# Gated long convolution and token MLP: the second forward transform stage in 64x32 tiles, the first in row pairs, and one shuffle per row pair

## The chip, the cores and the metric

The kernel runs on one core of one Trainium2 chip. The metric is the device time of one execution in microseconds; lower is better. Of several runs the median is given. The profile is of one further execution, and its span (first to last instruction on the core) is a little shorter than its device time.

## The reference, cut to what matters

S = 2048 positions, D = 448 channels, F = 1792, one batch, bf16 inputs.

```python
def A(q, k, v, shift_k, ssm_k, ssm_D):
    k_pad = pad(k, 3 rows in front)
    k_shift = sum(k_pad[:, t:t + S, :] * shift_k[:, 3 - t] for t in range(4))
    kv = k_shift * v
    kv_f = rfft(pad(kv, to 2 * S), along S)
    kf_f = rfft(pad(ssm_k, to 2 * S), along S)
    y = irfft(kv_f * kf_f)[:S].astype(bf16)
    return q * (y + kv * ssm_D)

def B(x, w1, b1, w2, b2):
    h = layernorm(x)                               # over D
    u = gelu(einsum("bsd,sf->bdf", h, w1) + b1)    # mixes positions
    return transpose(einsum("bdf,fs->bds", u, w2) + b2)

h = x + A(layernorm(x), k, v, shift_k, ssm_k, ssm_D)     # x is A_q
out = h + B(layernorm(h), w1, b1, w2, b2)
```

## The kernel before

The sequence is laid out as 128 partitions by R = 16 rows: position 16 q + r sits in partition q, row r. The long convolution is done as a transform of length 4096 in two forward stages, a product, and two inverse stages, all as matmuls with tables of sines (`E`, `FW`, `MA`, `MB`, `MN`, `ET`). DB is the 896 bytes of one row of 448 bf16 channels.

In order of the data: `emit_kT` transposes the filter `ssm_k` into `KT`; `emit_kv` does the short convolution (transposes L947, matmuls L973, and a multiply by v on DVE, L988) and leaves kv in `V`. `emit_stage1` (L1030) runs once for the filter (tag k, from KT) and once for kv (tag u, from V). For each group i of four rows it makes four frequency quarters `jh`. For one quarter eight matmuls (L1040) of 128x32 weights go to the four column tiles of the array, one row per tile, the two parts x (real and imaginary) to two PSUM banks; a bank pair of 128x896 is then copied to SBUF by ACT or DVE (L1050; L1048 for the first group of k, where `DR` adds the coefficient ssm_D to the filter's transform). After every second quarter three DMAs (L1056) move the result from partitions that stand for (row, frequency) to the layout of stage 2: partitions 0 to 31 and 96 to 127 by POOL, 32 to 95 by SP. They write half of the columns of 32 partitions of `TK` or `TU`.

`emit_stage2` (L1067) takes two frequency columns j at a time. For each part h it has four matmuls of 128x64 weights (L1075), two column tiles, and the bank pair goes back into T in place (`evac`, L719 on ACT and L722 on DVE without a scale, L720 and L723 with the scale of the k path). `emit_products_i1` multiplies the two transforms on DVE (L1108, 128x1792) and does the first inverse stage (L1120) with two row tiles; its result is evacuated to TU, and DMAs (L1144, and L1133 for the last pair) shuffle it back to `TZ`. `emit_i2` (L1240 and the normalisation after it) and `emit_mlp` (L1365, L1375, L1387) follow. `emit_warm` and `dummy` (L1154, L1006) are matmuls whose result is not used. BN statistics of q (L1180, L1182) are computed on DVE in between, and small steps of the normalisation on POOL (L1185, L1188, L1197).

The order of work is set by a planner in the kernel (`_Sched`). Every step of a stage has a rank, written out by hand in `WHEN`; an engine takes, of the operations that are ready in the planner's own clock, the one with the lowest rank. `WHERE` names for each evacuation that may run on either engine whether it is ACT, DVE, or left to the planner. The resulting order is then fixed in the program of each engine, and semaphores hold each instruction until its operands are there. PSUM's eight banks are handed out in pairs; the results of stage 1 go through a ring of buffers (`gring`) in the regions of `MR` and `X`, and the load of q into X waits for the last shuffle of u.

The lines of before that the change touches most:

```python
for i in range(R // 4):                       # stage 1, L1032
    for jh in range(4):
        c0 = 64 * (jh & 1) + 32 * (jh >> 1)
        for x in range(2):
            for q, r in enumerate((4 * i, 4 * i + 2, 4 * i + 1, 4 * i + 3)):
                ...
for h in range(2):                            # stage 2, L1070
    for c in range(2):
        for par in range(2):
            j = 2 * jj + par
            ... FW[:, 64 * c:64 * c + 64], T[:, j, h, :] -> PS[64 * par:64 * par + 64, b.slots[c]]
```

Of the kernel before, what the change touches and what calls it, by code (L numbers as in the profile page):

```python
# [12 lines left out]
    "dummy": (283,),  # L13
    "tables": (138, 234, 288, 20, 81, 325, 139, 217,),
    "loads": (91, 107, 134, 143, 231, 216, 80, 297, 0, 238, 183, 285, 228, 299, 145,),
    "kv": (290, 148, 151, 174, 63, 282, 100, 192, 205, 47, 18, 112, 141, 45, 207, 160, 233,),
    "kT": (201, 13, 14, 175, 200, 130, 54, 53,),
    "k1": (132, 135, 152, 226, 122, 144, 165, 213, 68, 51, 154, 167, 89, 168, 262, 336,),
    "k2": (23, 150, 83, 97, 224, 227, 140, 153, 258, 248, 180, 195, 169, 219, 338, 235,),
    "u1": (71, 86, 116, 123, 46, 82, 176, 221, 117, 215, 261, 316, 173, 184, 277, 278,),  # L20
    "xload": (156, 298, 314, 302,),
    "bias": (75, 171,),
    "q": (271, 208, 318, 93, 268, 185, 279, 280, 264,),
    "u2": (133, 142, 220, 210, 241, 249, 64, 114, 159, 196, 137, 189, 1, 115, 252, 251,),
    "i1": (179, 121, 99, 3, 190, 96, 186, 149, 188, 240, 203, 202, 128, 92, 212, 95,),
    "ct": (36, 187, 87, 300,),
    "xn": (257, 17, 6, 222, 161, 317,),
    "w1a": (329, 239, 230, 55,),
    "w1b": (306,),
    "warm": (291, 307, 265, 27, 292, 147, 330, 320, 5, 304, 270, 38, 19, 315, 284, 62, 333, 327, 105, 118, 191, 295,  # L30
        324, 259, 56, 8, 332, 113, 236, 273, 206, 198, 182, 274,),
    "i2": (260, 69, 103, 39, 15, 31, 293, 28, 108, 242, 90, 84, 88, 331, 22, 197, 204, 33, 110, 237, 164, 323, 256,
        310, 73, 214, 223, 170, 44, 79, 157, 177, 16, 211, 328, 281, 131, 250, 4, 247, 158, 294, 109, 40, 29, 104,
        34, 243, 267, 129, 98, 287, 70, 178, 67, 162, 246, 120, 155, 2, 125, 11, 229, 42, 253, 272, 59, 124, 119,
        266, 12, 78, 194, 276, 127, 41, 313, 10, 102, 61, 255, 21, 37, 66, 24, 232, 199, 321, 312, 76, 308, 296, 52,
        111, 303, 163, 319, 58, 65, 339, 209, 26, 326, 337, 289, 85,),
    "w2": (146,),
    "mlp": (218, 57, 136, 126, 77, 30, 25, 48, 60, 9, 305, 72, 166, 245, 301, 172, 50, 181, 418, 419, 420, 421, 422,
        423, 424, 425, 426, 427, 428, 429, 430, 431, 432, 433, 434, 435, 436, 437, 438, 439,),
}  # L40
WHERE = {
    "kv": "ddaffffa",
    "kT": "fadfdddd",
    "k1": "fafaafaffaff",
    "k2": "dfdffadaafdafada",
    "u1": "fffaafadaaddafaa",
    "bias": "a",
    "u2": "fdaafafaaaaadafa",
    "i1": "affadfaaffdaffaf",
    "ct": "ffda",  # L50
    "xn": "aaff",
    "i2": "aaffaadafddf",
# [518 lines left out]
def _build(nc, A_q, A_k, A_v, A_shift_k, A_ssm_k, A_ssm_D, B_w1, B_b1, B_w2, B_b2, out):  # L571
# [5 lines left out]
    Bsz, S, D = A_q.shape  # L577
    F = B_w1.shape[1]
    assert Bsz == 1 and S == 2048 and D == 448 and F == 1792 and A_shift_k.shape[-1] == 4
    R = 16  # L580
    NFC = F // 128
    EPS = 1e-5
    DB = 2 * D
# [42 lines left out]
    with ctx:  # L626
# [47 lines left out]
        o_GR = (o_WR, o_WR + 8 * DB, o_X, o_X + 8 * DB)  # L674

        def GR_(s):
            return view(o_GR[s], [R // 4, 2, D])
# [13 lines left out]
        gring = _Pool(4)  # L691
# [36 lines left out]
        def emit_tables():  # L728
# [47 lines left out]
            op("pool", lambda e, W: e.iota(chi, [[0, 2], [1, 4], [0, 16]], base=0, channel_multiplier=0),  # L776
               w=[(o_gc + 512, 512)], n=128, est=190.0)
            for a, b_, c_ in ((0, 112, 14), (112, 128, 2)):
                op("pool", lambda e, W, a=a, b_=b_, c_=c_: e.iota(gcm[:, a:b_], [[0, 8], [512, c_]], base=512 * 14 * (a > 0),
                                                                 channel_multiplier=0),  # L780
                   w=[(o_gc + 1536 + 4 * NB, 512, "gm")], n=128, est=190.0)
                op("pool", lambda e, W, a=a, b_=b_, c_=c_: e.iota(chm[:, a:b_], [[0, 2], [1, 4], [0, c_]], base=0,
                                                                 channel_multiplier=0),
                   w=[(o_gc + 2048 + 4 * NB, 512, "cm")], n=128, est=190.0)
            for k, (b0, st_) in enumerate(((2048, -2048), (2048, 2048), (0, 2048))):
                for a, b_ in (((0, 128),) if k == 0 else ((0, 112), (112, 128))):
                    op("pool", lambda e, W, k=k, b0=b0, st_=st_, a=a, b_=b_: e.iota(
                        cph[:, 128 * k + a:128 * k + b_], [[st_, 2], [0, (b_ - a) // 2]], base=b0, channel_multiplier=0),
# [8 lines left out]
            fields = ((5, 12), (0, 2048), (9, 3), (7, 15), (7, 15), (11, 3), (13, 1), (11, 2))  # L797
# [66 lines left out]
        def emit_loads():  # L864
# [11 lines left out]
            for i, (src, c) in enumerate((("k", 3), ("k", 0), ("v", 0), ("k", 1), ("v", 1), ("k", 2), ("v", 2), ("v", 3))):  # L876
# [9 lines left out]
            op(Dq, lambda e, W: e.dma_start(DR[0:16, :], A_ssm_D.rearrange("(a d) -> a d", a=1).broadcast_to([16, D])),  # L886
               w=[(o_DR, DB)], dmab=16 * DB)
# [142 lines left out]
        def emit_stage1(src, o_src, T, o_T, tag):  # L1030
            shuf[tag] = []
            for i in range(R // 4):  # L1032
                g = _Buf(gring)
                for jh in range(4):
                    sch.t0 = T_K1 + T_DK1 * (4 * i + jh) if tag == "k" else T_U1 + T_DU1 * (4 * i + jh)
                    b = _Buf(psum, 2)
                    c0 = 64 * (jh & 1) + 32 * (jh >> 1)
                    for x in range(2):
                        for q, r in enumerate((4 * i, 4 * i + 2, 4 * i + 1, 4 * i + 3)):
# [13 lines left out]
                    if jh % 2 == 0:  # L1053
                        continue
                    for q_, a, nu in (("pool", 0, 8), ("pool", 96, 8), ("sp", 32, 16)):
                        shuf[tag].append(op(q_, lambda e, W, g=g, i=i, a=a, nu=nu, jh=jh: e.dma_start(  # L1056
                            T[a + i:a + i + 4 * nu - 3:4].rearrange("p (j k) c d -> p j k c d", k=4)[:, :, jh - 1:jh + 1]
                            .rearrange("p j k c d -> p j (k c d)"),
                            GR_(g.slots[0])[a:a + 4 * nu, jh - 1:jh + 1].rearrange("p k c d -> p (k c d)")),
                           br=[g], w=[(o_T + (4 * j + jh - 1) * 2 * DB, 4 * DB, tag) for j in range(4)],  # L1060
                           dmab=4 * nu * 4 * DB, keng=nu, rate=350.0))
# [5 lines left out]
        def emit_stage2(T, o_T, scale):  # L1067
            for jj in range(R // 2):
                bs = [_Buf(psum, 2) for _ in range(2)]
                for h in range(2):  # L1070
                    sch.t0 = (T_K2 if scale else T_U2) + T_D2 * (2 * jj + h)
                    for c in range(2):
                        for par in range(2):
                            j = 2 * jj + par
                            op("pe", lambda e, W, b=bs[h], h=h, j=j, c=c, par=par: e.matmul(  # L1075
                                PS[64 * par:64 * par + 64, b.slots[c], 0:D], FW[:, 64 * c:64 * c + 64], T[:, j, h, :],
                                start=True, stop=True),
                               r=r_fw + [(o_T + (2 * j + h) * DB, DB)], bw=[bs[h]], n=D, est=94.5, mode=2)
                for h in range(2):
                    i = 2 * jj + h  # L1080
# [17 lines left out]
        def emit_products_i1():  # L1098
            for jj in range(R // 2):
                ms = []  # L1100
                for h in range(2):
                    i = 2 * jj + h
                    sch.t0 = T_I1 + T_DI1 * i
# [12 lines left out]
                for h in range(2):  # L1116
# [7 lines left out]
                    evac(lambda jj=jj, h=h: TU[:, 2 * jj:2 * jj + 2, h, :], lambda b=bs[h]: Ppair(b),  # L1124
# [325 lines left out]
```

## Time and profile before

| | |
|---|---|
| device time, median of 3 runs | 179.49 us (178.26, 179.49, 179.64) |
| device time of the profiled execution | 178.13 us |
| span of the profiled execution | 175.9 us |
| granted TensorE clock | 1.000 throughout |
| busy: PE, DVE, ACT, POOL | 166.1, 102.0, 92.2, 63.3 us |
| stage 1 evacuations on ACT, L1050 | 24, 919 ns each |
| products, L1108 | 16, 1080 ns each |
| POOL issues of stage-1 shuffles, L1056 | 32, 553 ns each |
| stage 1 matmuls, L1040 | 256, from 13.7 to 43.2 us |
| stage 2 matmuls, L1075 | 128, from 36.0 to 66.8 us |
| inverse stage 1 matmuls, L1120 | 128, from 53.6 to 73.0 us |

The busy time of PE is taken from matmuls that overlap and whose ends are modelled, so 94% of the span is not the peak of the array; the time from one matmul's start to the next tells more. An evacuation is one ACT or DVE instruction that reads two PSUM banks; successive ones overlap a little, so the distance between their starts is somewhat less than the mean duration. A DMA issue counts as busy on POOL, and for SP it stands in the queue's own record (SPq).

### The profile page before, as it was taken

How to read it: one execution, taken by the hardware profiler on the slowest of the kernel's cores; microseconds unless marked ns; L12 is line 12 of the kernel's file. 1: busy time of each engine (PE TensorE's matmuls, PEld its weight loads, DVE VectorE, ACT ScalarE, POOL GpSimd, SP SyncE). 2: the span in 40 equal slices, each digit the busy share in tenths (PEclk: the TensorE clock that was granted, in tenths of full speed). 3: DMA queues.
4: the chain of work that ended last, by engine and by line, in shares of the span. 5: the costliest groups of instructions: out<-in, count | busy, mean ns of one | idle time of the engine just before them, and what ended most of it. 6: DMA issues, size and time to landing. Idle time of an engine off the chain costs nothing.

```text
span 175.9 us, 3619 instructions
## 1 busy us (share of the span) xinstructions
PE 166.1 (94%) x1445; PEld 95.6 (54%) x1445; DVE 102.0 (58%) x189; ACT 92.2 (52%) x131; POOL 63.3 (36%) x157
## 2 busy tenths in 40 slices
PE   6999999879979999998999999999999999999994
PEld 2786745342323333644544455555557777777784
DVE  6995696848999999998998860000001231331331
ACT  3799958888979999966982656412120000000000
POOL 8576628670600643894888760000000000000000
PEclk9999999999999999999999999999999999999999
DMA  5999855992849386569999999910000111011111
GB/s 174 416 334 332 268 165 201 325 352 71 250 98 383 110 214 198 167 179 390 383 396 405 421 419 417 419 77 0 0 4 0 52 52 52 16 40 52 52 52 52
DMA packets 15444, 35.13 MB, mean 200 GB/s; under 512 B 3820, under 2 KB 9484, under 8 KB 15428
## 3 DMA queue, kind: packets, MB, share of 16 engines
q1 hardware_dynamic: 12164, 28.00, 43.4%
q0 software_dynamic: 3072, 6.80, 12.6%
q8 instruction: 11, 0.18, 0.4%
q10 hardware_dynamic: 192, 0.11, 0.2%
q14 instruction: 5, 0.04, 0.1%
HBM read 22.05 MB, written 1.84 MB: 136 GB/s over the span
## 4 chain that ended last, share of the span: by engine, by line
PE 68%; ACT 10%; POOL 7%; DMA 7%; DVE 4%; issue 2%; DVEq 0%; POOLq 0%
PE ps L1387 24%; PE ps L1375 12%; PE ps L1365 9%; ACT arena L719 8%; DMA arena<-arena 7%; PE ps L1040 4%; PE ps L1006 3%; POOL arena L1056 3%; PE ps L947 3%; PE ps L1240 3%; PE ps L1075 2%; PE ps L1019 2%; PE ps L973 2%; PE ps L1120 2%; DVE arena L1259 1%
## 5 line engine op out<-in xcount | busy, mean ns | idle before, releaser
L1390 DVE SCALAR_TENSOR_TENSOR arena<-ps,arena 128x448 bf16<-128x448 f32 (+2 forms) x17 | 11.1, 656 | 57.4 <-PE ps L1387 57.4
L1387 PE MATMUL ps<-arena 128*128 128x448 bf16 (+2 forms) x238 | 42.7, 342 | 0.0
L1387 PEld LDWEIGHTS ps<-arena 128*128 128x128 bf16 x238 | 33.3, 145 | 9.5
L719 ACT CAST arena<-ps 128x896 bf16<-128x896 f32 (+1 forms) x29 | 23.4, 948 | 1.2 <-PE ps L1075 1.1
L1365 PE MATMUL ps<-arena 128*128 128x448 bf16 x112 | 22.9, 353 | 0.4 <-DVE arena L1318 0.4
L1056 POOL DMA_DIRECT2D arena<-arena x32 | 17.5, 553 | 14.1 <-ACT arena L1050 12.9
L1050 ACT CAST arena<-ps 128x896 bf16<-128x896 f32 x24 | 20.3, 919 | 3.8 <-PE ps L1040 3.5
L1375 PE MATMUL ps<-arena 128*128 128x448 bf16 x112 | 21.8, 353 | 0.0
L1075 PE MATMUL ps<-arena 128*64 128x448 bf16 x128 | 15.8, 360 | 3.4 <-DMA arena<-arena 1.8
L1355 ACT ACTIVATE arena<-ps,arena 128x448 bf16<-128x448 f32 x14 | 8.6, 633 | 19.4 <-PE ps L1375 17.7
L1108 DVE TENSOR_TENSOR arena<-arena 128x1792 bf16<-128x1792 bf16 x16 | 16.7, 1080 | 0.2
L1365 PEld LDWEIGHTS ps<-arena 128*128 128x128 bf16 x112 | 10.6, 98 | 11.5 <-DVE arena L1318 2.5
L1375 PEld LDWEIGHTS ps<-arena 128*128 128x128 bf16 x112 | 10.9, 98 | 10.2
L1040 PE MATMUL ps<-arena 128*32 128x448 bf16 x256 | 15.3, 356 | 0.4 <-DVE arena L988 0.3
L1120 PE MATMUL ps<-arena 64*128 64x448 bf16 x128 | 14.0, 352 | 1.0 <-ACT arena L719 0.9
L1144 POOL DMA_DIRECT2D arena<-arena x14 | 8.2, 588 | 17.4 <-ACT arena L719 16.6
L1075 PEld LDWEIGHTS ps<-arena 128*64 128x64 f16 x128 | 5.7, 108 | 12.8 <-ACT arena L719 3.6
L1287 ACT ACTIVATE arena<-arena 128x448 bf16<-128x448 f32 x14 | 8.0, 575 | 5.9 <-DVE arena L1259 5.7
L988 DVE TENSOR_TENSOR arena<-ps,arena 128x512 bf16<-128x512 f32 (+1 forms) x16 | 9.0, 617 | 2.7 <-PE ps L973 2.7
L1120 PEld LDWEIGHTS ps<-arena 64*128 64x128 f16 x128 | 5.1, 94 | 9.5 <-ACT arena L719 5.0
L719 ACT COPY arena<-ps 128x1024 bf16<-128x1024 bf16 (+1 forms) x9 | 8.9, 1019 | 0.9 <-PE ps L1154 0.6
L1040 PEld LDWEIGHTS ps<-arena 128*32 128x32 f16 x256 | 5.1, 95 | 7.8 <-DVE arena L988 1.9
(94 smaller groups left out, 207.0 us busy)
## 6 DMA issues: line engine op xcount, KB each, us to landing
arena<-in_B_w_dram SPq DMA_DIRECT2D x8, 896.0 KB, 12.0
arena<-in_B_w_dram SPq DMA_DIRECT2D x2, 2048.0 KB, 17.1
arena<-arena SPq DMA_DIRECT2D x16, 224.0 KB, 3.7
arena<-arena POOLq DMA_DIRECT2D x32, 112.0 KB, 3.8
arena<-in_B_w_dram SPq DMA_DIRECT2D x2, 1536.0 KB, 18.7
arena<-arena POOLq DMA_DIRECT2D x14, 196.0 KB, 4.6
arena<-in_A_k_dram SPq DMA_DIRECT2D x4, 448.0 KB, 5.7
arena<-in_A_v_dram SPq DMA_DIRECT2D x4, 448.0 KB, 9.0
```

The costliest lines, as they stand in the source:

```text
L719: return e.copy(out=dst(), in_=src())
L988: return e.tensor_tensor(out=v, in0=u.rearrange("p t (r d) -> p t r d", d=64), in1=v, op=ALU.mult)
L1040: op("pe", lambda e, W, b=b, r=r, q=q, x=x, c0=c0: e.matmul(PS[32 * q:32 * q + 32, b.slots[x], 0:D], E[:, 2 * r + x, c0:c0 + 32], src[:, r ...
L1050: return e.copy(out=dst, in_=Ppair(b)) if W == "act" else e.tensor_copy(out=dst, in_=Ppair(b))
L1056: shuf[tag].append(op(q_, lambda e, W, g=g, i=i, a=a, nu=nu, jh=jh: e.dma_start(T[a + i:a + i + 4 * nu - 3:4].rearrange("p (j k) c d -> p ...
L1075: op("pe", lambda e, W, b=bs[h], h=h, j=j, c=c, par=par: e.matmul(PS[64 * par:64 * par + 64, b.slots[c], 0:D], FW[:, 64 * c:64 * c + 64], ...
L1108: op("dve", lambda e, W, m=m, i=i: e.tensor_tensor(out=MR(m.slots[0]).rearrange("p (x y) d -> p x y d", x=2), in0=TU[:, i].unsqueeze(2).br ...
L1120: k = op("pe", lambda e, W, b=bs[h], m=ms[h], par=par, t=t, tab=tab, xy=xy, P=P: e.matmul(Pb(b, par), tab[P, :], MR(m.slots[0])[P, xy, :], ...
L1365: op("pe", lambda e, W, r=r, fc=fc, b=bs[fc]: e.matmul(Pb(b), W1A[:, r, 128 * fc:128 * fc + 128], Q[:, r, :], start=(r == 0), stop=(r == R ...
L1375: op("pe", lambda e, W, r=r, fc=fc, b=b: e.matmul(Pb(b), W1B[:, r, 128 * (fc - n0):128 * (fc - n0) + 128], Q[:, r, :], start=(r == 0), sto ...
L1387: op("pe", lambda e, W, r=r, fc=fc, b=b, d0=d0, d1=d1: e.matmul(Pb(b)[:, d0:d1], W2[fc // 7][:, fc % 7, r:S:R], G[:, fc, d0:d1], start=(fc ...
L1390: op("dve", lambda e, W, r=r, b=b, A=A, d0=d0, d1=d1: e.scalar_tensor_tensor(out=X[:, r, d0:d1], in0=Pb(b)[:, d0:d1], scalar=bm[:, r:r + 1 ...
```

## The change

Stage 1 takes rows in pairs (i of eight). The four column tiles now hold two rows in two frequency halves, and two quarters `jh` finish a pair. One DMA per row pair moves all 128 partitions at once to sixteen partitions of T, at steps of eight, over all columns; even pairs go by SP, odd ones by POOL. The ring has eight buffers of half the size. Stage 2 pairs column jj with jj + 8. Each matmul takes 64 partitions and 32 weight columns, so that eight tiles (two row tiles, four column tiles) hold the two columns, the two parts h and the two halves t. The products and the inverse stage follow the new numbering, the tables get their constants for it, `DR` is filled in two places (one more DMA), and `WHEN` and `WHERE` are new lists.

```diff
 WHEN = {
...
-    "k1": (132, 135, 152, 226, 122, 144, 165, 213, 68, 51, 154, 167, 89, 168, 262, 336,),
-    "k2": (23, 150, 83, 97, 224, 227, 140, 153, 258, 248, 180, 195, 169, 219, 338, 235,),
-    "u1": (71, 86, 116, 123, 46, 82, 176, 221, 117, 215, 261, 316, 173, 184, 277, 278,),
+    "k1": (105, 154, 129, 182, 62, 181, 50, 124, 223, 242, 99, 102, 188, 200, 127, 227,),
+    "k2": (90, 337, 244, 245, 296, 297, 247, 264, 47, 5, 79, 72, 211, 246, 204, 89,),
+    "u1": (210, 259, 217, 243, 27, 91, 73, 132, 100, 183, 117, 164, 144, 163, 190, 209,),
...
-        o_GR = (o_WR, o_WR + 8 * DB, o_X, o_X + 8 * DB)
+        o_GR = tuple(o + 4 * DB * s for o in (o_WR, o_X) for s in range(4))
...
-        gring = _Pool(4)
+        gring = _Pool(8)
...
-            op(Dq, lambda e, W: e.dma_start(DR[0:16, :], A_ssm_D.rearrange("(a d) -> a d", a=1).broadcast_to([16, D])),
-               w=[(o_DR, DB)], dmab=16 * DB)
+            for h in range(2):
+                op(Dq, lambda e, W, h=h: e.dma_start(DR[64 * h:64 * h + 16, :],
+                                                     A_ssm_D.rearrange("(a d) -> a d", a=1).broadcast_to([16, D])),
+                   w=[(o_DR, DB, "dr")], dmab=16 * DB)
...
-            for i in range(R // 4):
+            for i in range(R // 2):
                 g = _Buf(gring)
-                for jh in range(4):
+                pi = 4 * (i & 1) + (i >> 1)
+                for jh in range(2):
...
                     b = _Buf(psum, 2)
-                    c0 = 64 * (jh & 1) + 32 * (jh >> 1)
                     for x in range(2):
-                        for q, r in enumerate((4 * i, 4 * i + 2, 4 * i + 1, 4 * i + 3)):
+                        for q in range(4):
+                            r = 2 * i + (q & 1)
+                            c0 = 64 * ((q >> 1) ^ x) + 32 * jh
...
-                    if jh % 2 == 0:
-                        continue
-                    for q_, a, nu in (("pool", 0, 8), ("pool", 96, 8), ("sp", 32, 16)):
-                        shuf[tag].append(op(q_, lambda e, W, g=g, i=i, a=a, nu=nu, jh=jh: e.dma_start(
-                            T[a + i:a + i + 4 * nu - 3:4].rearrange("p (j k) c d -> p j k c d", k=4)[:, :, jh - 1:jh + 1]
-                            .rearrange("p j k c d -> p j (k c d)"),
-                            GR_(g.slots[0])[a:a + 4 * nu, jh - 1:jh + 1].rearrange("p k c d -> p (k c d)")),
-                           br=[g], w=[(o_T + (4 * j + jh - 1) * 2 * DB, 4 * DB, tag) for j in range(4)],
-                           dmab=4 * nu * 4 * DB, keng=nu, rate=350.0))
+                q_ = ("sp", "pool")[i & 1]
+                shuf[tag].append(op(q_, lambda e, W, g=g, pi=pi: e.dma_start(
+                    T[pi:pi + 121:8].rearrange("p (j k) c d -> p j (k c d)", k=2),
+                    GR_(g.slots[0]).rearrange("p k c d -> p (k c d)")),
+                   br=[g], w=[(o_T, 32 * DB, tag)], dmab=128 * 4 * DB, rate=350.0))
...
                 bs = [_Buf(psum, 2) for _ in range(2)]
+                for c in range(2):
+                    sch.t0 = (T_K2 if scale else T_U2) + T_D2 * (2 * jj + c)
+                    for h in range(2):
+                        for F_ in range(2):
+                            for t in range(2):
+                                j = jj + 8 * F_
+                                g0 = 64 * (t ^ h) + 32 * F_
+                                P = slice(64 * t, 64 * t + 64)
+                                op("pe", lambda e, W, b=bs[h], h=h, j=j, c=c, g0=g0, P=P, t=t: e.matmul(
+                                    PS[g0:g0 + 32, b.slots[c], 0:D], FW[P, 32 * c:32 * c + 32], T[P, j, h, :],
+                                    start=True, stop=True, tile_position=(64 * t, g0)),
+                                   r=r_fw + [(o_T + (2 * j + h) * DB, DB)], bw=[bs[h]], n=D, est=23.6, mode=5)
                 for h in range(2):
-                    sch.t0 = (T_K2 if scale else T_U2) + T_D2 * (2 * jj + h)
-                    for c in range(2):
-                        for par in range(2):
-                            j = 2 * jj + par
-                            op("pe", lambda e, W, b=bs[h], h=h, j=j, c=c, par=par: e.matmul(
-                                PS[64 * par:64 * par + 64, b.slots[c], 0:D], FW[:, 64 * c:64 * c + 64], T[:, j, h, :],
-                                start=True, stop=True),
-                               r=r_fw + [(o_T + (2 * j + h) * DB, DB)], bw=[bs[h]], n=D, est=94.5, mode=2)
-                for h in range(2):
-                    i = 2 * jj + h
+                    i = jj + 8 * h
...
-                    evac(lambda jj=jj, h=h: TU[:, 2 * jj:2 * jj + 2, h, :], lambda b=bs[h]: Ppair(b),
+                    evac(lambda jj=jj, h=h: TU[:, jj:jj + 9:8, h, :], lambda b=bs[h]: Ppair(b),
...
```

In the changed file the lines after the tables stand a few numbers later: the multiply L988 is L991, stage 1's matmul L1040 is L1045 and its evacuations L1048 and L1050 are L1053 and L1055, its shuffle L1056 is L1059, stage 2's matmul L1075 is L1079, and the later lines are four numbers on (L1108 is L1112, L1120 is L1124, L1185 is L1189, L1240 is L1244).

## The prediction

> **What bounds the kernel now.** I read the page's 40 slices first, then the chain that ended last, then the busy times by stretch, then the timelines of ACT and DVE for the stretches in which the change lies.
>
> From 79.72 us on nothing of the change is met. The chain is PE from there to the end (L1240, L1365, L1375, L1387), so what the change is worth is the time at which the first L1240 can start, and that is set by a landing:
>
> ```profile
> 46.77 4.02 DMA arena<-arena
> 50.83 0.99 PE ps L1075 x8
> ...
> 76.30 3.37 DMA arena<-arena
> 79.72 1.69 PE ps L1240 x8
> ```
>
> The reader should see two hinges in the columns start, length: the last first-stage shuffle of the u path lands at 50.79, the second stage of u starts at 50.83; the last inverse shuffle lands at 79.67. So the front has two halves: start to 50.8, and 50.8 to 79.7.
>
> The second half is bound by the engines that empty PSUM, not by PE:
>
> ```profile
> 51.81 19.53 ACT L719 CAST arena<-ps 128x896 bf16<-128x896 f32 x24 [1.09 <-PE ps L1075]
> 50.89 9.44 DVE L1108 TENSOR_TENSOR arena<-arena 128x1792 bf16<-128x1792 bf16 x9
> 52.00:56.00 4.00, 3.14 (x30) 1.07 (x28) 4.00 (x4) 4.00 (x6) 0.00 (x0) 1.00 0.94 350
> 64.00:68.00 4.00, 3.74 (x36) 1.21 (x32) 4.00 (x7) 4.00 (x7) 1.43 (x3) 1.00 0.75 213
> ```
>
> ACT runs 24 evacuations without a hole (0.81 us each); in the stretches (columns: length, PE, PEld, DVE, ACT, POOL busy, clock, DMA) DVE and ACT stand at 4.00 of 4.00. PE's busy time is no peak, and its own waits in the list of waits are for ACT ("PEld ps L1120 <- ACT arena L719: 5.0, 11, 0.7").
>
> The first half does have holes in both evacuating engines:
>
> ```profile
> 20.00:24.00 4.00, 3.74 (x109) 2.92 (x102) 3.54 (x7) 2.11 (x4) 1.94 (x4) 1.00 0.89 273
> 24.00:28.00 4.00, 4.00 (x77) 1.69 (x77) 3.25 (x5) 3.90 (x5) 1.08 (x2) 1.00 0.26 89
> 28.00:32.00 4.00, 3.99 (x90) 2.29 (x90) 3.14 (x5) 3.25 (x5) 3.56 (x7) 1.00 0.79 261
> 32.00:36.00 4.00, 2.56 (x56) 0.95 (x49) 3.05 (x5) 3.27 (x5) 2.62 (x6) 1.00 0.99 349
> 36.00:40.00 4.00, 3.75 (x52) 2.17 (x52) 2.17 (x3) 3.27 (x5) 2.43 (x5) 1.00 0.97 352
> 40.00:44.00 4.00, 3.85 (x58) 1.09 (x56) 3.22 (x6) 3.54 (x5) 0.30 (x1) 1.00 0.12 40
> 48.00:52.00 4.00, 3.52 (x32) 1.35 (x30) 3.97 (x4) 2.78 (x4) 0.00 (x0) 1.00 0.48 114
> ```
>
> Between 20 and 80 us ACT is idle some 6.3 us and DVE 6.5 us. Their work is not changed, so closing every hole would save (6.3 + 6.5) / 2 = 6.4 us; that is the ceiling.
>
> Last, the price of a shuffle: POOL needs 0.54 us per issue and there are four in a row behind the last evacuations, which end at 45.03:
>
> ```profile
> 45.11 0.54 POOL arena L1056
> 45.70 1.07 POOL arena L1056 x2
> DMA to landing us min/median/max: 2.2/3.7/5.7
> ```
>
> From 45.03 to 50.79 are 5.76 us.
>
> [...]in the single records of the trace its four 128x32 tiles (L1040) start 3 to 4 ns apart and the next set of four follows 0.19 us later, so four do run at once.[...] The new stage 2 writes both row tiles into one bank, in different quadrants; no line of before shows that case (L973 and L1120 put their row tiles into different banks).[...] the stretch from 44 to 48 us, with the last groups in flight, moved 245 GB/s where that from 36 to 40 us moved 352.
>
> **The change part by part.**
> Matmuls. Stage 1 keeps 128 matmuls and 16 evacuations of 128x896 for k and for u. Stage 2 goes from 8 matmuls in sets of two (four sets of 0.19 us, 0.76 us for a pair of j; 0.95 with the tail) to 16 in sets of eight: if a set costs what one of four costs, 2 x 0.19 = 0.38 us. PE saves 0.38 us x 16 = 6 us over both paths. In u's second stage this is hidden behind ACT and DVE and worth nearly nothing; in the first half PE stands ahead of them.
>
> Order. The program of the changed kernel has all of kT and 88 of 128 k1 matmuls ahead of the convolution (before: 64), then 128 convolution matmuls in one run (before 108), and all but 8 of u1 ahead of all but 48 of k2 (before 48 u1 matmuls stand behind half of k2). I follow the two queues.
> DVE: by 13.3 us it has done the tables and kT copies in before; now 7.8 us stand between these and the first multiply (four 1.08 stage-1 evacuations, three 0.67 copies, 1.21, 0.26), from 14.8 when a k1 result can be there, so the multiplies L991 start at 22.4 (before 20.46). Then 12 x 0.58, 4 evacuations x 1.02, 4 x 0.58, 3 x 1.02, which is 38.9, and eight k2 evacuations to 47.1.
> ACT: it is out of work near 22, because convolution groups hold the PSUM pairs until DVE has multiplied them; from 25.5 on it has 13 stage-1 evacuations x 0.86, 36.7; 1 us for holes; 3 of k2 x 0.84; the last of u1 0.86. That ends at E = 41.1; I take 41.5, bounds 39.5 and 46 (before 45.03).
>
> Shuffles. 32 issues on POOL and 16 on SP become 8 and 8, same bytes. POOL saves 24 x 0.54 us, of which only the four behind the last evacuations were on the path. A new one is 448 KB with 16 first-dimension steps. An undisturbed SP shuffle of half that size took 2.4 us in the trace (issue 43.44, landing 45.83), its transfer 0.75 of it, so 2.4 + 0.75 = 3.15; an undisturbed POOL one of 112 KB took 2.86, so some 3.6. The last one then lands at 41.5 + 3.7 = 45.2 with a little queueing; bounds 3.2 and 5.8 after E.
>
> The barrier. Each new shuffle writes 16 partitions of the whole T, so no second-stage matmul can go before the eighth has landed. Before, half the columns were free one half-group earlier, and four u2 evacuations (ACT 48.90, DVE 48.89) ran ahead of 50.79. Now all 32 u2 and i1 evacuations come after. What hides the gap is k2: five of its eight jj steps stand behind the last u1 matmul, with about 4 ACT and 8 DVE evacuations.
>
> From the landing to the last i1 evacuation. ACT: 0.45 for the first matmuls, 28 x 0.814, two copies of L719 128x1024 at 0.95 = 25.2 (before 75.17 - 50.79 = 24.4). So 45.2 + 25.2 = 70.4. DVE: 47.1 + 16 products x 1.05 + 4 evacuations x 1.02 + 2 x 0.55 = 69.1, then 0.9 PE and 0.9 ACT: 70.9. The later rules: 70.9 against 75.17, which is 4.3 us earlier.
>
> Last inverse shuffle. Ahead of its POOL issues stands one L1189 (0.23) where L1185, L1197 and L1188 stood: 0.3 earlier. Behind: 11 BN statistics and their aggregates fill DVE until 76, as they did until 79.3.
> i2. DVE gets one more gate (0.68) and one more BN statistic (0.6) there; half of it on the path, +0.6. Holes that I can't see, +0.5. The one DMA added for DR and the iota fields lie in the start-up.
> Sum: -4.3 - 0.3 + 0.6 + 0.5 = -3.5 us. The profiled execution took 178.13 (span 175.9 and 2.2 around it), so 174.6. The runs shown have their median at 179.49, 1.4 above it; I give the forecast on that median: 176.0.
>
> **The rivals.**
> R1, the gain is lost in the first half (no change). For: DVE starts to multiply 2 us later than before and then has no slack for 25 us, and ACT waits 3.5 us for PSUM. If E stays at 45.03, only the shuffles (-2.2) count against the barrier (+0.8), -0.3 and +1.1: about -0.6, 178.9. Against: PE's 24 more k1 matmuls go out earlier, and their evacuations are done.
> R2, nearly all holes close: -6, 173.5. For: DVE's queue has none by my count. Against: ACT's 3.5 us.
> R3, slower: the eight tiles take turns, two row tiles in one bank being held apart. It sits in k2 and u2. If sixteen matmuls go in pairs, a jj step costs 8 x 0.19 = 1.5 us: 48 k2 matmuls ahead of the last u1 put E at 44.8, the other five steps hold PE until 52.3, then 8 x 1.5 of u2 and 16 x 0.84 of i1 bring the last evacuation to 78.6, 3.4 us later than 75.17: 182.9. It decides from 1.4 us per step, because ACT's 24.7 us less 13.4 of i1 leave 11.3 for eight. Sets of four (0.76) would cost nothing that ACT doesn't hide. Against: the other tilings here run at full set rate.
>
> **How the numbers follow.** Forecast 0.53, R1 0.20, R2 0.10, R3 and whatever else puts E past 48 0.17. About 1% is what a measurement of this kernel can tell from no change. The forecast's spread (E 39.5 to 46, landing 3.2 to 5.8) gives -6 to +1 us; 173.0 takes in R2, and 181.0 takes in R1 and the nearer half of the slow cases. Faster by over 1% 0.63, same 0.20, slower 0.17.
>
> **What would show it.** Right: stage-2 sets of eight with 0.19 us between sets; the last u shuffle landing near 45 and the first u2 matmul right behind it; ACT without holes from there for 25 us; the first inverse L1244 near 76. Wrong: a step of 16 matmuls over 1.4 us (R3); the last u1 evacuation at 45 or later with DVE full and ACT idle around 22 to 26 (R1); a POOL shuffle landing over 5 us after its issue; a granted clock under 1.

## The result and the profile after

The changed kernel takes 180.8 us (median of 16 runs, 178.75 to 182.81), the kernel before 178.91 on the same chip (16 runs): a ratio of 1.0106, 95% interval 1.0065 to 1.0147. It is 1.9 us slower where 3.5 us faster was forecast. Ratios are formed from the runs that lie within 1.5% of a kernel's fastest. The profiled execution took 182.01 us (span 180.2), which is 1.2 us above the median, against 178.13 (175.9) before: distances in its trace hold some of that 1.2 us too.

The chain that ended last, columns start, length, what:

```profile
33.41 9.04 DMA arena<-arena
42.45 0.09 issue
42.54 1.08 PE ps L1079 x21
...
46.76 0.81 ACT arena L1055
47.58 5.72 DMA arena<-arena
53.30 0.04 issue
53.34 1.28 PE ps L1079 x16
...
81.03 3.16 DMA arena<-arena
84.24 1.69 PE ps L1244 x8
```

There are three hinges now where there were two. The new one is the first: the last shuffle of the k path takes 9.04 us, and all of k2 waits for it. The last u shuffle lands at 53.30 (before 50.79), the first L1244 starts at 84.24 (before L1240 at 79.72). From there to the end of the span are 96.0 us (before 96.2), so what lies behind that point takes as long as before.

The timelines show who waits (start, length, group, idle time ahead of it and its releaser), PE's first:

```profile
42.54 1.51 PE L1079 MATMUL ps<-arena 64*32 64x448 bf16 x32 [4.51 <-DMA arena<-arena]
45.55 0.88 PE L1045 MATMUL ps<-arena 128*32 128x448 bf16 x8
53.34 1.71 PE L1079 MATMUL ps<-arena 64*32 64x448 bf16 x32 [1.45 <-DMA arena<-arena]
```

ACT's:

```profile
37.97 1.71 ACT L1055 CAST arena<-ps 128x896 bf16<-128x896 f32 x2 [0.56 <-PE ps L1045]
43.60 1.73 ACT L720 ACTIVATE arena<-ps 128x896 bf16<-128x896 f32 x2 [3.92 <-PE ps L1079]
```

DVE's:

```profile
35.93 3.08 DVE L1055 CAST arena<-ps 128x896 bf16<-128x896 f32 x3
43.53 2.09 DVE L723 TENSOR_SCALAR arena<-ps 128x896 bf16<-128x896 f32 x2 [4.51 <-PE ps L1079]
```

All but the last u1 evacuation are done at 39.7. PE, ACT and DVE stand for some 4 us ahead of k2, which starts with k's landing, and the last eight u1 matmuls (L1045 at 45.55) stand behind k2 in PE's program.

The shuffles' own line, L1059:

```profile
DMA to landing us min/median/max: 4.4/7.1/12.5
```

Three stretches (length, PE, PEld, DVE, ACT, POOL busy, clock, DMA share, GB/s):

```profile
32.00:36.00 4.00, 3.85 (x92) 2.34 (x88) 3.63 (x7) 2.53 (x4) 1.05 (x2) 1.00 1.04 236
36.00:40.00 4.00, 2.02 (x40) 0.57 (x32) 3.02 (x4) 3.12 (x4) 0.53 (x1) 1.00 0.97 230
52.00:56.00 4.00, 2.14 (x40) 0.66 (x40) 2.42 (x3) 2.26 (x3) 0.00 (x0) 0.63 0.44 130
```

The landing was 2.2/3.7/5.7 before. The DMA engines are as full as before (share 1.04 and 0.97, before 0.99 and 0.97) but move 230 to 236 GB/s where they moved 349 to 352. And the granted clock, the share of full speed that TensorE is allowed, is no longer 1.00 throughout: its records stand at 0.50 from 42.8 to 46.2 and from 53.1 to 59.9 us (hence the 0.63 in the last line).

### The profile page after: what moved, and what is told of

Same layout as the page of the kernel before. It is cut to its first block, busy times and chain, and to the rows that moved or that the text cites. A ratio compares the mean times of both kernels' runs of the same rounds, so it can differ in the third digit from the quotient of the medians.

```text
span 180.2 us, 3821 instructions
## 1 busy us (share of the span) xinstructions
PE 165.1 (92%) x1573; PEld 93.8 (52%) x1573; DVE 105.8 (59%) x192; ACT 89.5 (50%) x128; POOL 46.4 (26%) x133
## 4 chain that ended last, share of the span: by engine, by line
PE 58%; DMA 14%; DVE 14%; ACT 5%; POOL 4%; issue 2%; SPq 1%; DVEq 0%; POOLq 0%
PE ps L1391 23%; PE ps L1379 12%; DMA arena<-arena 10%; PE ps L1369 6%; DMA arena<-in_A_ssm_k_dram 5%; PE ps L1045 4%; DVE arena L1112 4%; PE ps L1079 3%; ACT arena L719 3%; PE ps L1244 2%; DVE arena L1263 2%; DVE arena L991 2%; PE ps L950 2%; PE ps L1124 2%; PE ps L976 2%
## 5 line engine op out<-in xcount | busy, mean ns | idle before, releaser
L1079 PE MATMUL ps<-arena 64*32 64x448 bf16 x256 | 15.0, 439 | 8.0 <-DMA arena<-arena 6.0
L1055 ACT CAST arena<-ps 128x896 bf16<-128x896 f32 x21 | 18.1, 917 | 6.3 <-PE ps L1045 6.3
L1112 DVE TENSOR_TENSOR arena<-arena 128x1792 bf16<-128x1792 bf16 x16 | 16.7, 1085 | 1.1 <-ACT arena L719 0.6
L1045 PE MATMUL ps<-arena 128*32 128x448 bf16 x256 | 15.1, 361 | 0.8 <-DVE arena L991 0.4
L1148 POOL DMA_DIRECT2D arena<-arena x14 | 8.2, 590 | 29.0 <-ACT arena L719 28.5
L1124 PE MATMUL ps<-arena 64*128 64x448 bf16 x128 | 14.4, 365 | 0.6 <-ACT arena L719 0.5
L1079 PEld LDWEIGHTS ps<-arena 64*32 64x32 f16 x256 | 3.7, 98 | 18.1 <-issue 5.7
L723 DVE TENSOR_SCALAR arena<-ps 128x896 bf16<-128x896 f32 x8 | 8.4, 1087 | 5.7 <-PE ps L1079 5.7
L1124 PEld LDWEIGHTS ps<-arena 64*128 64x128 f16 x128 | 5.5, 98 | 9.3 <-ACT arena L719 4.7
L719 ACT COPY arena<-ps 128x1024 bf16<-128x1024 bf16 (+1 forms) x10 | 10.0, 1028 | 0.3 <-issue 0.2
L1055 DVE CAST arena<-ps 128x896 bf16<-128x896 f32 x9 | 9.5, 1085 | 0.5 <-PE ps L1045 0.4
L720 ACT ACTIVATE arena<-ps 128x896 bf16<-128x896 f32 x8 | 7.0, 916 | 5.4 <-PE ps L1079 5.4
```

Source lines behind the costliest of these rows:

```text
L719: return e.copy(out=dst(), in_=src())
L723: return e.tensor_scalar(out=dst(), in0=src(), scalar1=scale, scalar2=None, op0=ALU.mult)
L1045: op("pe", lambda e, W, b=b, r=r, q=q, x=x, c0=c0: e.matmul(PS[32 * q:32 * q + 32, b.slots[x], 0:D], E[:, 2 * r + x, c0:c0 + 32], src[:, r ...
L1055: return e.copy(out=dst, in_=Ppair(b)) if W == "act" else e.tensor_copy(out=dst, in_=Ppair(b))
L1079: op("pe", lambda e, W, b=bs[h], h=h, j=j, c=c, g0=g0, P=P, t=t: e.matmul(PS[g0:g0 + 32, b.slots[c], 0:D], FW[P, 32 * c:32 * c + 32], T[P, ...
L1112: op("dve", lambda e, W, m=m, i=i: e.tensor_tensor(out=MR(m.slots[0]).rearrange("p (x y) d -> p x y d", x=2), in0=TU[:, i].unsqueeze(2).br ...
```

## The experiments

Four causes were open: the partitions that a shuffle writes (T1, called **ports** in the labels and the expectations), the place of the last u1 group in the program (T2), the clock (T3), and the size of a whole shuffle (T4). A fifth came up on the way: that everything hangs on the start of k2 (T5). The edits are shown in short form; where the targets move, the constants of the tables that follow them are not shown.

### Ports

A new shuffle writes sixteen partitions in steps of eight, over all 128; SP's DMA of before writes sixteen in steps of four, from 32 to 92. From 32 to 40 us the new targets move 230 to 236 GB/s and the old ones 349 to 352. That ports are the reason was my estimate; no trace shows a port, only the rate of each choice of partitions. Even shuffles write the partitions whose number is 0 to 3 modulo 8 and odd ones the others, and with both queues in flight the packets of both were slow (medians from 36 to 40 us: SP's, of 3584 bytes, 242 ns where they took 140 before, POOL's, of 7168, 495 where they took 276). No run here shows why.

**v1_ports** gives the changed kernel the old targets:

```diff
-  T[pi:pi + 121:8]                          # one DMA, pi = 4 * (i & 1) + (i >> 1)
+  T[32 + (i >> 1):...:4]                    # even i: SP, 16 partitions
+  T[(i >> 1):...:4], T[96 + (i >> 1):...:4] # odd i: POOL, two DMAs of 8 partitions
```

> The changed kernel with its eight-tile second stage, but with the shuffles' target partitions as in the kernel before: even i by one DMA to partitions 32 to 92 in steps of four, odd i by two DMAs of 8 partitions to 0 to 28 and 96 to 124; the tables' bit fields follow.[...] Order of all engines unchanged apart from the 8 additional DMA issues on POOL. Ports (T1): the windows from 32 to 40 us are back at about 350 GB/s instead of 230, median landing of a shuffle 3.5 to 4.5 us instead of 7.1, the last k shuffle lands by 38 instead of 42.5, the last u shuffle by 48 instead of 53.3, time 174 to 177. Program order alone (T2) or the plain size of the DMA (T4; the even half still goes in 448 KB pieces): landings of the even half stay at 7, k's last at 41 to 42.5, time 179.5 to 182. Clock alone (T3): no more than 0.5 us.

Measured: 179.29 us, ratio to before 1.0029 (1.0001 to 1.0058). Median landing 5.6 us, the last k shuffle at 41.46 instead of 42.45. Its busy times by stretch:

```profile
36.00:40.00 4.00, 2.23 (x44) 0.69 (x40) 3.24 (x4) 3.28 (x4) 0.47 (x1) 1.00 0.96 300
40.00:44.00 4.00, 1.91 (x48) 0.77 (x48) 1.57 (x2) 1.50 (x2) 1.77 (x4) 0.75 0.99 313
```

At a DMA share of 0.96 to 0.99 these are 300 to 313 GB/s (228 to 230 in the changed kernel, at 0.97 to 1.03): the targets count, but they returned some 0.8%. That is most of the loss against the kernel before, but the time is far from the 174 to 177 us expected for T1.

**e_half64** keeps the single DMA and moves it to sixteen partitions in steps of four, within one half of the 128:

```diff
-  pi = 4 * (i & 1) + (i >> 1);   T[pi:pi + 121:8]
+  pi = 64 * (i & 1) + (i >> 1);  T[pi:pi + 61:4]
```

> The changed kernel with one edit: a shuffle still is one DMA of 448 KB to 16 partitions, but to 0 to 60 in steps of four (even i) or 64 to 124 (odd i), instead of all of the 128 in steps of eight. The rows of the stage-2 input are permuted by it, so that part of the computation is changed; times and order of the engines are not.[...] Ports (T1): like the changed kernel, 230 GB/s, median landing 6.5 to 7.5 us, time 180 to 182. If it is the step of eight itself, or the spread over all partitions: 350 GB/s, landing 4, time 174 to 177. If it is the size of the DMA (T4): as slow as the changed kernel also, which v1_ports tells from T1.

Measured: 181.63, ratio 1.018 (1.010 to 1.026), median landing 7.7. The tables do not follow the new rows here, so part of what is computed differs; the work and its order do not. The step of eight and the spread over all partitions are not what costs.

**b_ports** is the mirror, in the kernel before:

```diff
-  (("pool", 0, 8), ("pool", 96, 8), ("sp", 32, 16))
+  (("pool", 64, 8), ("pool", 96, 8), ("sp", 0, 16))
```

> The kernel before with one edit, the mirror of v1_ports: its shuffles keep their sizes, their order and their sources' numbering, but SP's 16 partitions are now 0 to 60 in steps of four[...] instead of 32 to 92[...], and POOL's two pieces take 64 to 124. Ports (T1): the SP shuffles' packets, half of the bytes, take twice as long; the stretch from 32 to 40 us falls from 350 to between 230 and 270 GB/s, the last u shuffle lands 1 to 3 us later, time 0.5 to 1.5% above the kernel before. Size or pattern of the new shuffle (T4): no change, 350 GB/s.

Measured: 180.69, ratio 1.0108 (1.0039 to 1.0176). The edit moves what each DMA reads along with what it writes: SP's now reads partitions 0 to 63, where it read 32 to 95. So it shows what the choice of partitions for each DMA costs, and not the targets alone; for these the two kernels above stand. That choice costs a kernel with none of the change's other parts as much as the whole change did. The median landing went from 3.7 to 5.5 us, and the stretch from 36 to 40 us moves 265 GB/s (before 352) at a full share:

```profile
36.00:40.00 4.00, 2.16 (x22) 1.32 (x24) 1.09 (x1) 2.92 (x4) 2.78 (x6) 1.00 1.00 265
```

In the single DMA records of the stretch from 36 to 40 us, the median time of a packet of 3584 bytes is 140 ns in the kernel before, 242 in the changed one, 240 in e_half64, 206 in b_ports and 140 in v1_ports.

### Program order and clock

**e_order** plans all of u1 ahead of k2 and makes k2's matmuls wait for all of u1's:

```diff
-  ("k1", ...), ("k2", ...), ("u1", ...)
+  ("k1", ...), ("u1", ...), ("k2", ...)     # and k2's matmuls: safter = all of u1
```

> The changed kernel with the last u1 groups planned and issued on PE ahead of the k2 matmuls, so that they do not stand behind the wait for k's shuffles. Program order (T2): last u1 evacuation at 42 to 43.5 instead of 47.55, last u landing at 48 to 49, time 175 to 177. Ports (T1): u1 does end early, but its shuffles queue on the same slow writes as k's, so the last u landing comes only 1 to 2.5 us earlier (51 to 52.5); time 178.5 to 180; the windows stay at about 230 GB/s.

Measured: 196.29, ratio 1.1003 (1.0927 to 1.1079). The planner gave the later work another order too, and the first second-inverse matmul starts at 95.15. It decides nothing about T2.

**e_u1first** moves only what it should, in the finished order:

```diff
+  late = last 8 u1 matmuls; ev = their evacuation; sh = its shuffle
+  order = head + late + [ev, sh] + rest      # head ends ahead of the first k2 operation
```

> The changed kernel with only the last eight u1 matmuls moved ahead of the first k2 matmul on PE, their PSUM pair swapped with that k2 group's, and the evacuation and its shuffle moved with them; all else in the order of the changed kernel. Program order (T2): last u1 evacuation at 40.5 instead of 47.55, last u landing earlier by 3 or more, time 176 to 178. If the chain runs through k instead (T5: k's last landing at 42.5, then the 16 k2 evacuations of about 1.2 us a pair, which end at 52 to 53 whatever u does): the u landing comes 0.5 to 2.5 us earlier but u2 still starts its evacuations at 52.5 to 53.5, time 179.5 to 181.

Measured: 179.87, ratio 1.0062 (1.0012 to 1.0113). PE still waits 2.67 us for k, until 41.34, and the second inverse stage starts at 81.36. T2 comes to some 0.4%, which is not clear of the noise (the intervals overlap); the bulk stays with k, as T5 has it.

**v1_u1first** adds the old targets.

> v1_ports[...] with the last eight u1 matmuls and their evacuation moved ahead of k2 as in e_u1first. T5, chain through k's landing: the same as v1_ports within 0.4%, 178.5 to 179.7, because u2's evacuations still stand behind k2's. T2 added to ports: 176 to 177.5.

Measured: four runs from 176.33 to 180.69, median 179.48; the ratio 0.992 (0.9836 to 1.0004) rests on the lower two of them. That is too wide to tell from v1_ports.

**e_fill** keeps PE busy in the hole:

```diff
+  for _ in range(20):                        # ahead of the first k2 matmul's wait
+      nc.tensor.matmul(PS[:, slot, 0:D], DUM[:, 0:128], DUM, start=True, stop=True)
```

> The changed kernel with 20 unused 128x448 matmuls (about 0.19 us each, 3.8 us) on PE right ahead of the first k2 matmul's wait for k's shuffles, in a hole of 4.5 us, to keep PE busy there. Clock (T3): the granted clock stays at 0.95 to 1.0 from 40 to 60 us, u2 and the first inverse matmuls run at full speed, the end comes 1.5 to 2.5 us earlier (178 to 179.5). Ports (T1) with a path through the DMAs: the landings stay (42.5 and 53), u2 to the last first-inverse evacuation 26.7 falls by at most 1 us; time 180 to 181.

Measured: 180.75, ratio 1.0139 (1.0060 to 1.0219). The clock held to 53.7 us and fell then, behind the wait for u; k landed at 42.04 and u at 52.50 (42.45 and 53.30 in the changed kernel). Filling the hole did not by itself make the kernel faster.

**v5_fill** has the old targets, u1 first, and 12 unused matmuls; **e_u1f_fill** the same with the changed kernel's targets.

> v1_u1first[...] with 12 unused 128x448 matmuls (2.3 us) on PE right ahead of the first k2 matmul's wait, in a hole of 2.5 us. v1_u1first took 176.33 in a run with the clock granted in full over the whole span, 178.38 at 0.990, and 180.6 at 0.971. Clock (T3, added to ports and order): the clock stays at 0.99 to 1.0 in every run, k2's 16 evacuations take 8.5 to 9 us instead of 10.2, time 176 to 177, faster than the kernel before. If the clock only went along with something else: 178.5 to 180 as before, at a clock of 0.99 or more.

> The changed kernel[...] and both other edits: last u1 group ahead of k2 and 12 unused matmuls ahead of k2's wait. Beside v5_fill it shows what ports alone are worth once order and clock are mended. If ports, order and clock add up (ports about 1.3 us in v1_ports, order 0.8 in e_u1first): 178 to 179. If the clock is nearly all: as v5_fill, 176 to 177.

Measured: 178.54, ratio 1.0012 (0.9988 to 1.0037), lowest of 14 runs 177.99; and 179.62, ratio 1.0076 (1.0053 to 1.0099). With the clock at 0.999 or 1.000 in nearly all runs of v5_fill, the 176.33 did not come again: the clock was not what made it, and what did is open. With the two mended, the old targets are worth 0.6%. The clock by itself is worth nothing that shows: e_u1f_fill, with a mean clock of 1.000 in its profiled execution, is no faster than e_u1first with 0.981 (ratio 1.0062). Now k's landing is the only long wait; v5_fill's chain:

```profile
33.03 8.81 DMA arena<-arena
41.89 0.97 PE ps L1105 x32
...
81.16 1.69 PE ps L1270 x8
```

ACT's timeline:

```profile
51.64 21.39 ACT L744 CAST arena<-ps 128x896 bf16<-128x896 f32 x26
```

It runs without a hole from 51.64, right behind k2's last evacuation, and its last stage evacuation ends at 76.6: 25.0 us, where the prediction has 25.2 from u's landing.

**v5_dbl** issues each k2 matmul twice.

> v5_fill with every k2 matmul issued twice (its result is the same), so that a k2 step costs PE 0.76 us instead of 0.38, as much as in the kernel before, and PE idles less between 42 and 52 us. If k2's speed on PE hardly matters because evacuation (1.04 us a step on DVE) is the bound and the clock is what the idle time costs: within 0.5% of v5_fill, or faster if v5_fill still loses clock. If k2's delay from landing to evacuation is what counts, the additional 0.2 to 0.4 us ahead of each evacuation add up to 1.5 to 3 us: 178 to 180.

Measured: 181.52, ratio 1.0158 (1.0106 to 1.0210), against 1.0012: some 2.6 us for some 0.38 us more (two sets of 188 ns, as in v9_split) in each of eight steps. k2 is on the path, and there the PE time that the eight tiles save does pay.

### Whose bytes are ahead of k's

**v3_plan** is v1_ports with the planner's priorities searched anew, with slower shuffles.

```diff
-  dmab=128 * 4 * DB, rate=350.0              # whole shuffle, one after the other
+  dmab=8 * nu * 4 * DB, keng=nu, rate=300.0  # and 159 of 340 ranks in WHEN changed
```

> v1_ports with a new plan: priorities of the planner's steps searched anew with the shuffles charged at 235 to 270 GB/s and shared between the two queues, instead of 350 one after the other. Same instructions, another order. If the loss came from a program order that was laid out for shuffles faster than they are (T5 and T1 together): last k landing ahead of 40 and used at once, time 174.5 to 177.5. If something else sets the end: as v1_ports, 178.5 to 179.5.

Measured: 178.98, ratio 1.0008 (0.9966 to 1.0051). k2 started at 40.71, but the last inverse shuffle took longer (chain):

```profile
70.95 2.52 issue
...
75.84 5.03 DMA arena<-arena
80.92 1.69 PE ps L1237 x8
```

It was issued 0.5 us earlier than before's (76.30), and landed 1.2 us later: the gain was lost at the next wait.

**v7_kdma** is v5_fill with two u shuffles (POOL) taken out from beside k's last ones:

```diff
+  mv = first four u shuffles' DMAs on POOL   # two shuffles of two DMAs
+  ops[i].eng = "sp"; placed behind k's last shuffle in SP's order
```

> v5_fill[...] with two u shuffles that stood on POOL's queue beside and ahead of k's last ones moved to SP's queue behind k's last shuffle; nothing else moves. In v5_fill k's last shuffle is issued at 33.0 and takes 8.8 us because it shares the DMA engines with those two. If k's landing is the hinge (T5): k lands at 37 to 39 instead of 41.8, k2's evacuations end at 48 to 49.5 instead of 51.7, u2 starts there, the first second-inverse matmul at 77.5 to 79 instead of 81.2; time 175 to 177, faster than the kernel before (178.3). If the bytes only change their order and u lands later for it: u's last landing after 50, time 178 to 179.5.

Measured: 179.64, ratio 1.0068 (1.0044 to 1.0092). In the single records k has landed at 38.7. But the u shuffles hold their ring buffers longer, and ACT's queue stands for that, with k2's evacuations behind it:

```profile
41.25 2.52 ACT L1086 CAST arena<-ps 128x896 bf16<-128x896 f32 x3 [4.08 <-DMA arena<-arena]
43.65 2.81 ACT L752 ACTIVATE arena<-ps 128x896 bf16<-128x896 f32 x3
```

**v6_split** is v5_fill with each shuffle in two pieces (and ten unused matmuls), **v8_both** adds v7's order.

```diff
-  T[...].rearrange("p (j k) c d -> p j (k c d)", k=2)                 # behind both evacuations
+  T[...].rearrange("p (j k) c d -> p j k c d", k=2)[:, :, jh]         # behind each, L1058
```

> v5_fill with each shuffle issued in two pieces, one behind each of its two evacuations (224 KB with pieces of 1792 B per partition, instead of 448 KB with 3584 B behind the second). If whole shuffles cost by their size (T4), the first half of the data moves about 1 us earlier and the last one is shorter: k's last landing at 39.5 to 40.8 instead of 41.8, time 176.8 to 178. If not: 178 to 179.5, or more, because there are 16 more issues on POOL.

> v6_split and v7_kdma together. If both count: 174.5 to 176.5. If the order of the bytes alone counts: as v7_kdma.

Measured: 178.93, ratio 1.0043 (1.0021 to 1.0066), and 179.08, ratio 1.0048 (1.0022 to 1.0074). In single records v6_split's last k shuffle lands at 39.5 and v8_both's at 37.3, and k2 starts at the same time in both, because I had put other work there (v8_both, PE):

```profile
39.30 0.56 PE L1076 MATMUL ps<-arena 128*32 128x448 bf16 x8 [1.05 <-DVE arena L1086]
39.79 2.06 PE L1452 MATMUL ps<-arena 128*128 128x448 bf16 x10
41.78 1.09 PE L1113 MATMUL ps<-arena 64*32 64x448 bf16 x32
```

L1452 are the unused matmuls. The two earlier mends, u1 first and the unused matmuls, now held k2 back.

**v9_kq** is v8_both without both mends, **v9_kq_u1** without the unused matmuls alone.

> v1_ports with shuffles in two pieces as in v6_split and four u shuffles on SP's queue behind k's last as in v8_both, but with the order of PE and ACT as in the changed kernel (k2's first 48 matmuls ahead of the last u1 group) and no unused matmuls. In v8_both k landed at 37.3, but PE still stood before the last u1 group and then ran 2.0 us of unused matmuls, and k2 started only at 41.85, so its early landing was not used. T5 (the hinge is when k2 starts): k2 starts at 37.5 to 38.5, the last u1 evacuation ends at 41 to 42 as the prediction had it, k2's evacuations end at 48 to 49, u2 starts at 48.5 to 50.5; time 174.5 to 177, faster than the kernel before. If the ring slots that u's shuffles hold stop ACT whatever k does (v7_kdma: 4.1 us): 178 to 179.5.

> v8_both without its unused matmuls. k lands at 37.3; PE is through with the last u1 group at 39.9 and can start k2 there instead of at 41.85. T5: 2 us earlier than v8_both, 176.5 to 177.5. Otherwise as v8_both, 178.5 to 179.5.

Measured: 178.74, ratio 1.0026 (1.0003 to 1.0048), and 178.96, ratio 1.0036 (1.0012 to 1.0061). In v9_kq eight k2 matmuls start at 38.45, then PE waits 2.70 us for a PSUM pair, whose evacuation on ACT waits for a ring buffer for 2.97 us (3.39 us in v9_kq_u1). In this ring, to reorder the bytes is to move the wait from k's landing to the ring.

**v9_split** is v1_ports with the two pieces and nothing else. **e_split8** is the changed kernel with the two pieces, on its own targets. PE, DVE and ACT run in the changed kernel's order in both.

> v1_ports with only the shuffles cut into two pieces; order and queues as in the changed kernel. Whole shuffles cost by their size (T4): k's last landing at 39 to 40 instead of 41.5, time 177 to 178.3. Order of the bytes is what counts: 178.5 to 179.5 as v1_ports.

> The changed kernel with only the shuffles cut into two pieces of 224 KB, one behind each evacuation; its targets stay as they are, 16 partitions in steps of eight[...]. PE, DVE and ACT run in the same order as in the changed kernel and in v9_split. It completes the square of ports and size: changed kernel 180.8 (1.0106 of the kernel before), ports alone (v1_ports) 1.0029, both (v9_split) 0.9936. If the two add up, size alone gives 0.9 to 1.0%: a ratio of 1.000 to 1.003, k's last landing at 41 to 41.5. If the pieces only help once the ports are free[...]: 1.007 to 1.012, landing at 42 to 43.

Measured: v9_split 176.93 us, ratio 0.9936 (0.9901 to 0.9972), some 0.6% faster than the kernel before; e_split8 179.74, ratio 1.0085 (1.0055 to 1.0115). The square, as ratios to the kernel before, with k's last landing:

| | the changed kernel's targets | the old targets |
|---|---|---|
| whole, 448 KB | 1.0106, 42.45 us | 1.0029, 41.46 us |
| two pieces of 224 KB | 1.0085, 41.70 us | 0.9936, 39.72 us |

Pieces alone return 0.2% (the intervals overlap), the old targets alone 0.8%, both 1.7%. In e_split8 the DMA engines are full from 32 to 44 us (share 1.01 to 1.07), and in its chain k's last piece, of half the size, still takes 8.29 us, where the whole shuffle took 9.04; in v9_split it takes 5.24. Not all that v9_split gains on v1_ports is k's landing, which came 1.7 us earlier: PE's hole ahead of k2 shrank from 3.31 to 1.48 us, and the clock stayed at 0.999 (0.980 there). How the gain divides between them is not shown. v9_split's chain:

```profile
34.48 5.24 DMA arena<-arena
39.72 0.20 issue
39.92 0.96 PE ps L1081 x30
...
75.75 2.96 DMA arena<-arena
78.76 1.69 PE ps L1246 x8
```

### T5 in one table

First k2 matmul, first second-inverse matmul, and the distance (us, from PE's timelines), with the mean clock of the execution:

| kernel | k2 | inverse | distance | clock |
|---|---|---|---|---|
| changed | 42.54 | 84.24 | 41.7 | 0.972 |
| e_fill | 42.09 | 83.73 | 41.6 | 0.981 |
| v1_ports | 41.55 | 82.71 | 41.2 | 0.980 |
| e_split8 | 41.80 | 81.92 | 40.1 | 0.981 |
| e_u1f_fill | 42.40 | 81.33 | 38.9 | 1.000 |
| v5_fill | 41.89 | 81.16 | 39.3 | 1.000 |
| v6_split | 41.79 | 80.65 | 38.9 | 1.000 |
| v9_split | 39.92 | 78.76 | 38.8 | 0.999 |

At full clock the distance is 38.8 to 39.3 in these four, with the old targets and with the new: the end follows k2's start. It is not so for every order: v7_kdma, where ACT stands for the ring, and v3_plan, with its own plan, have 40.2 at full clock. The kernels that lost clock need 1 to 3 us more than the four; in the first two the late u landing adds to it, since u2 starts with it there.

The clock fell around PE's holes. Its records in the changed kernel stand at 0.50 for 3.41 and 6.83 us, and these two stretches come with waits of 4.51 and 1.45 us, one in e_u1first with 2.67, one in e_fill with 1.58, while v9_split's wait of 1.48 us cost no clock (1.00 in every stretch from 28 to 52 us). How much idle time it takes is not shown here.

## Why the prediction was wrong

**Right:** the sets of eight (in v9_split, at full clock, the eight of k2's first set start within 41 ns, both row tiles in one bank, and the next sets 188, 376 and 565 ns after it; rival R3 fell), the start of DVE's multiplies (22.65, predicted 22.4), the end of DVE's u1 evacuations (39.0, predicted 38.9; ACT's but one at 39.7, predicted 37.7), the 25.2 us of u2 and the first inverse stage (25.0 in v5_fill), and all that follows L1244.

Three of the four listed signs of error came true: a POOL shuffle landing over 5 us after its issue, a clock under 1, and R1's. The last u1 evacuation ended at 47.6, with DVE full and ACT idle from 23.0 to 26.5. But R1's reason is not what made it late, since all the others were done at 39.7. That 180.8 lies under the 181.0 of the forecast's range is luck: the spread was reckoned too narrow, since its late end (46 + 5.8, then 25.2 and the remaining terms) comes to 2.6 us slower and not 1, and k's landing is not in it.

**The step that failed** is "Shuffles". It priced a 448 KB shuffle by adding a second half of 0.75 us to an undisturbed one (whose packets stand in the trace from 44.63 to 45.50, 0.87 us), 3.15 us on SP and some 3.6 on POOL, 3.7 with queueing, at most 5.8. Measured are 4.4 to 12.5, median 7.1. The SP price came from a DMA to the old targets, whose packets took 140 ns, and was carried to the new ones, where they took 242; and several shuffles are in flight at once, so what counts is the rate at which the queue drains (230 GB/s), not the time of one. The second is the larger part: with the old targets (v1_ports) the median still is 5.6, and its last shuffle, with little beside it, took 3.5.

**The step that this pulled down** is "The barrier", with the order part's k2. The barrier was weighed for u alone, and k2 was named as what hides it. But k2 stands behind the same barrier. The count of DVE's queue had k2's evacuations start at 38.9; they start at 43.53, 4.6 us late. From there to L1244 the prediction has 37.1 us (76 less 38.9), the trace 40.7, 3.6 more. Of these 2.9 go with the clock and the late u (41.7 from k2's start in the changed kernel, 38.8 in v9_split); the other 0.7 are not accounted for. E followed: 47.55 and not 41.5, outside its bounds, because the last u1 matmuls stand behind 48 k2 matmuls in PE's program. The prediction saw them there and charged them PE time only, not k2's wait.

What remains open: with targets, pieces and clock mended, v9_split gains 0.6% where the forecast was 2%. Its k2 starts at 39.92, some 2 us later than the forecast needs, with 320 GB/s moving from 40 to 44 us; to send k's bytes ahead of u's ran into the ring (v7_kdma, v9_kq, v9_kq_u1). Whether a larger ring would free the rest was not tried, nor was a kernel without the barrier.

## What to carry to other kernels

Price an SBUF-to-SBUF shuffle by the bytes in flight beside it and by the GB/s that was measured for its own choice of partitions (here 230 against 350), not by one undisturbed landing. When one transfer takes the place of several, ask which consumers stood behind the pieces: each of them now waits for the whole, also the one that you count on as cover. A mend that fills a hole (unused matmuls, other work moved in) can become the bound as soon as the hole's cause is mended, as in v8_both.

## Of the hardware, not expected

The DMA engines moved a third less at the same share of 1.0: the slow targets show in the GB/s beside it (230 against 350), not in the share. A packet of 3584 bytes took 140 ns in the kernel before and 242 in the changed one (medians from 36 to 40 us). Cutting the shuffles' runs from 3584 to 1792 bytes cost no bandwidth that the stretches show (312 and 320 GB/s in v9_split from 36 to 44 us, 300 and 313 in v1_ports); with the changed kernel's targets it raised it (273 to 297 in e_split8 from 32 to 44 us, 228 to 236 in the changed kernel).
